# Four attention layers on one core: scores of two tiles issued together in the first stage, and the first chunk projected in blocks

## The chip, the core and the metric

The kernel runs on one core of a Trainium2 chip. The core has a matrix engine (PE in the profile; its weight loads are the row PEld), a vector engine (DVE), a scalar engine (ACT), GpSimd (POOL) and SyncE (SP), which issues transfers. The engines run at the same time, each through its own queue of instructions in order, and wait for each other through semaphores. PE writes to PSUM, eight banks of 128 x 512 float32; the other engines carry results from there to SBUF. The metric is the device time of one execution in microseconds (us).

## What is computed

```
x = x + A(layernorm(x));  x = x + B(layernorm(x))
x = x + A(layernorm(x));  x = x + B(layernorm(x))

A, B: q, k, v = x @ wqkv, 32 heads of 20 columns, S = 2048, D = 640
      p = softmax(q k^T / sqrt(20));  (p v) @ wo
A:    key k counts for query q only if 0 <= q - k < 256
B:    all keys count
```

A and B have their own weights and are each used twice. So there are four layers, 0 to 3; layers 0 and 2 are windowed, 1 and 3 full. All operands of the matmuls are bfloat16.

## The kernel before

The 2048 rows are four chunks of 512 columns (`c` = 0 to 3), and the 32 heads are eight groups of four (`g` = 0 to 7). Each head of a group has a strip of 32 partitions, of which 20 hold data. A **unit** is one layer, one chunk of queries and one group. Its scores are computed with keys on the partitions, in banks of 128 keys by up to 512 queries. A windowed unit of layer 0 has 12 banks: for each of four heads, three banks with masks. In chunk 0 these hold 512, 384 and 256 columns, in the later chunks 512.

The main loop (line 1389) goes over **tiles**. A tile is the next two or three banks of the list of units (`next_tile`, line 1344), and even and odd tiles have their own PSUM banks (line 1426). For each tile the code issues in this order: the scores on PE (line 1436); the exponential on ACT from PSUM to the tile `pt` (line 1462); some background work; the values of an earlier tile on PE (line 1495), accumulated in `op`; and the masks of the tile before on GpSimd and DVE (lines 1535 and 1546). The values come three tiles after the scores. When a unit ends, `op` goes to `on` (line 900), and tails scale it by the reciprocals of the sums.

**Background** is all that is not attention: layer norm (`t_ln`), values (`t_v`), projections of q and k (`t_block`, `t_qk_first`) and output projection (`t_out`). These are generators in the list `todo`, ordered by the unit that needs them less a lead (`push`, line 218). `background` (line 1373) advances them in every tile by a credit, 1.2 a tile while `state["unit"] < woven`; a projection costs 1.1, a piece of values 0.7. `require` (line 299) advances whatever is ahead in the list until a needed name is ready. Then `keep_clock` (line 681) adds matmuls that nobody reads (`unread`), where too little PE work was issued. While `state["unit"] < woven` (layer 0, chunks 0 and 1, sixteen units) the results of the background leave PSUM by ACT (`evac`, line 343), later by DVE.

For chunks after the first, q and k are projected in blocks of 128 columns, evacuated to a staging tile, stored to DRAM by a transfer that GpSimd issues (line 566), and read back per unit into strips of 32 partitions by eight transfers that SyncE issues (lines 802 and 803). `load_ahead` issues those of the next unit, when its blocks are ready and the buffers `qa` (4) and `ka` (18) have room. For chunk 0 of layer 0 this trip is left out: `t_qk_first` projects each group from weights that `get_w` (line 355) has spread to strips of 32 columns, with a GpSimd memset of the gaps and a DVE copy, and the evacuation goes straight to `qa` and `ka`.

The beginning is `first_ln` (line 1254): statistics of four row tiles on DVE, scale factors on GpSimd, normalization on ACT, transposes on PE, and copies to `xnT`. Filler matmuls (`warm`) stand between. Before it SyncE issues the loads of x (chunk 0), of the weights of layer 0, of x (chunks 1 to 3) and of the values' weights of the full layers. `other_constants` follows the first projection, and `t_zeros` fills buffers with zeros by transfers that GpSimd issues and then loads `wop`, the output weights.

Of the kernel before, what the change touches and what calls it, by code (L numbers as in the profile page):

```python
# [45 lines left out]
KEEP = 30  # L46
HALF = True
# [10 lines left out]
def kernel(  # L58
# [77 lines left out]
    for c in range(1, NC):  # L136
        nc.sync.dma_start(out=x_sb[:, 4 * c : 4 * c + 4, :], in_=xin[:, 4 * c : 4 * c + 4, :])
    nc.sync.dma_start(out=wv_sb[1][:], in_=wq_view[1][:, :, 2 * D : 3 * D])
# [32 lines left out]

    nc.vector.memset(ka_all[:, G:KA, :], 0.0)

    def other_constants():
        nc.vector.memset(op, 0.0)
# [3 lines left out]

# [38 lines left out]
    def push(name, gen, need, left):  # L218
        lead = 0
        if type(name) is tuple and need <= first_use(1, NC - 1, 0):  # L220
# [3 lines left out]
            if name[0] in ("k", "q"):  # L224
                lead = 7 if name[1] == 1 and name[-1] == 0 else 2

            if name[0] == "stats" or name[:2] == ("ln", 0):
                lead = 5
# [82 lines left out]
    def by_columns(out_, lhsT, rhs, start, stop):  # L311

        for j in range(4):
# [39 lines left out]
    padded = [0]  # L353

    def get_w(n, i):

        a = padded[0] % 8 * P
        padded[0] += 1
        t = wqk[:, :, a : a + P]
        tv = t.rearrange("p c (j m) -> p c j m", j=4)  # L360
        nc.gpsimd.memset(tv[:, :, :, DH:32], 0.0)
# [18 lines left out]
    def block_w(l, n, b):  # L380

        a = n * D + b * P
# [13 lines left out]
    def project(wt, xt, dst):  # L396
# [6 lines left out]
        evac(dst(), pq)  # L403
# [17 lines left out]
    def t_ln(l, c):  # L421
# [3 lines left out]
        users[l, c] = 9 if (l, c) == (0, 0) else (11, 12, 11, 11)[l]  # L425
# [50 lines left out]
    def t_v(l, c, halves):  # L476
# [9 lines left out]
        for i in range(4):  # L486
            if windowed:
# [46 lines left out]
    ka_free = deque(kas)  # L534
    qa_free = deque(qas)

    def t_qk_first(l, c, g):
# [13 lines left out]
        if g == G - 1:  # L551
            nc.sync.dma_start(out=wqk[:], in_=wq_view[1][:, :, 0 : 8 * P])
            nc.sync.dma_start(out=wqk_rest, in_=wq_view[1][:, :, 8 * P : 2 * D])
            ready.add("weights")

    def t_block(l, n, c, b):
# [5 lines left out]
        wt = block_w(l, n, b)  # L562
        yield from project(wt, xnT[l, c], staged)
        rows = slice(b * P, (b + 1) * P)
        dst = k_d[l][rows, c * C : (c + 1) * C] if n else q_d[l][c, rows, :]
        nc.gpsimd.dma_start(out=dst, in_=staging.pop())  # L566
        used(l, c)
        ready.add(("qk"[n], l, c, b))
# [68 lines left out]
    def push_layer(l, c):  # L637
# [18 lines left out]
        for g in range(G):  # L656
            for n in (0, 1):
                worder[l, n].append((n, g))
            push(("qk", l, c, g), t_qk_first(l, c, g), need[g], 2.2)
            if g == 0:  # L660
                push(("v", l, c), t_v(l, c, (0, 1)), need[0], 5.6)
# [118 lines left out]
    small_units = deque(u for u in units if u.windowed and (u.l, u.c) != (0, 0))  # L780
# [45 lines left out]
    def unit_needs(u):  # L826
        l, c, g = u.l, u.c, u.g
        if (l, c) == (0, 0):
            return [("qk", l, c, g)]
# [27 lines left out]
    def start_unit(u):  # L857
        for n in unit_needs(u):
            require(n)
        if (u.l, u.c) != (0, 0):  # L860
# [371 lines left out]
    def t_zeros():  # L1232

        z = ka_all[:, G : G + 4, :].rearrange("p a b -> p (a b)")
        yield ("wait", 4)
# [6 lines left out]
        load_wop(0, False)  # L1242
        for t in (*kts, *qts):
# [10 lines left out]
    def first_ln():  # L1254

        users[0, 0] = 9
# [9 lines left out]
        warm(14)  # L1266
# [23 lines left out]
        for i in range(4):  # L1290
# [8 lines left out]
            if i > 0:  # L1299
                trs.append(scale(i - 1))  # L1300
                warm((0, 3, 2)[i - 1])
        nc.vector.tensor_copy(out=xt[:, :, 0:P], in_=trs[0])
        trs.append(scale(3))
        warm(3)
        nc.vector.tensor_copy(out=xt[:, :, P : 2 * P], in_=trs[1])
        for n in (1, 0):
# [288 lines left out]
```

## Time and profile before

| | |
|---|---|
| time, median of 3 runs | 2161.81 us (2161.41 to 2163.21) |
| the profiled execution | 2161.74 us, span 2160.0 us |
| busy in the span | ACT 2088.0, PE 1926.8, DVE 1467.3, POOL 361.5 us |
| first projection, first exponential | at 13.26 and 16.73 us |
| evacuations leave ACT | from 148.85 us |

Times in the profile are us from the start of the span. A busy PE counts pipelined matmuls with modelled ends. A row of a group, wait or timeline names the line, the engine, the operation and the tile written and read; "x20" is a number of instructions. In the table by stretches each engine has its busy time in the stretch and its instructions, PEclk is the mean granted clock of PE, and then come the busy share of the DMA engines and their GB/s. A row of waits has the total, the number and the longest. In the timeline "SPq" is SyncE issuing, and a bracket gives the idle time before and what ended it.

### The profile page before, as it was taken

The numbers are of one execution on the slowest core, as the hardware profiler recorded it, in microseconds if no ns is written. First come the engines' busy times: TensorE is split into PE (matmuls) and PEld (weight loads), VectorE is DVE, ScalarE is ACT, GpSimd is POOL, SyncE is SP. The second block draws the span as 40 slices with busy tenths as digits, with TensorE's granted clock in tenths as the row PEclk, the third lists the DMA queues.
The fourth block names the chain that finished last, engine by engine and source line by source line (L and its number), as shares of the span: only waits on it lengthen the run. The fifth ranks groups of instructions, "written<-read, shape, count | busy, mean of one in ns | idle before, by whom it ended". The sixth has DMA issues, their size and how long they took to land. (4 is left out here: it accounts for less than half of the span.)

```text
span 2160.0 us, 73146 instructions
## 1 busy us (share of the span) xinstructions
PE 1926.8 (89%) x31790; PEld 757.8 (35%) x31791; DVE 1467.3 (68%) x2613; ACT 2088.0 (97%) x1717; POOL 361.5 (17%) x805
## 2 busy tenths in 40 slices
PE   8899999988889898888988989888898988888898
PEld 4444443433333333333333433342332222222222
DVE  6556665426666776776767743773588888987886
ACT  7889899999999999999999999999999999999997
POOL 6543434000022002400033001500000000000000
PEclk9999999999999999999999999999999999999999
DMA  6212122222110222111120122111111111111100
GB/s 204 65 54 75 54 62 69 67 63 59 55 42 27 63 53 69 38 31 48 50 83 27 33 60 75 33 45 52 54 57 44 36 36 42 32 33 39 44 27 17
DMA packets 81440, 114.33 MB, mean 53 GB/s; under 512 B 20990, under 2 KB 63070, under 8 KB 81118
## 3 DMA queue, kind: packets, MB, share of 16 engines
q1 hardware_dynamic: 71502, 81.06, 14.2%
q0 software_dynamic: 9616, 28.59, 3.8%
q8 instruction: 249, 4.08, 0.8%
q14 instruction: 73, 0.60, 0.1%
HBM read 76.58 MB, written 27.79 MB: 48 GB/s over the span
## 5 line engine op out<-in xcount | busy, mean ns | idle before, releaser
L1462 ACT ACTIVATE pt<-ps 128x1536 bf16<-128x1536 f32 (+2 forms) x1641 | 2054.0, 1417 | 38.5 <-PE ps L1436 28.9
L1436 PE MATMUL ps<-qt,kt 32*128 32x512 bf16 x3913 | 543.6, 384 | 62.8 <-ACT pt L1462 55.7
L315 PE MATMUL ps<-masks,ident 128*32 128x512 bf16 x5684 | 507.6, 384 | 94.7 <-ACT pt L1462 49.1
L1495 PE MATMUL ps<-pt,vt 128*21 128x512 bf16 x3784 | 377.1, 386 | 0.3 <-ACT pt L1462 0.2
L1436 PEld LDWEIGHTS <-kt 32*128 32x128 bf16 x3913 | 155.5, 91 | 460.1 <-issue 440.8
L315 PEld LDWEIGHTS <-ident 128*32 128x32 bf16 x5684 | 182.2, 94 | 283.4 <-issue 256.7
L1535 POOL TENSOR_SCALAR_AFFINE_SELECT pt<-pt 128x256 bf16<-128x256 bf16 (+2 forms) x508 | 219.0, 453 | 198.6 <-ACT pt L1462 185.8
L348 DVE CAST st<-ps 128x512 bf16<-128x512 f32 x134 | 92.6, 691 | 144.8 <-PE ps L315 144.5
L1495 PEld LDWEIGHTS <-vt 128*21 128x21 bf16 x3784 | 93.7, 89 | 254.2 <-issue 250.5
L315 PE MATMUL ps<-wop,on 128*32 128x320 bf16 x3712 | 160.7, 300 | 4.5 <-DVE x_sb L598 2.6
L1007 DVE TENSOR_SCALAR spare<-ps 128x512 int32<-128x512 f32 x200 | 137.2, 686 | 27.8 <-PE ps L989 24.1
L315 PEld LDWEIGHTS <-on 128*32 128x32 bf16 x5760 | 122.8, 95 | 62.3 <-issue 28.4
L1546 DVE TENSOR_TENSOR pt<-pt,masks 128x256 bf16<-128x256 bf16 (+3 forms) x270 | 117.0, 449 | 39.5 <-ACT pt L1462 37.6
L1436 PE MATMUL ps<-qa,ka 32*128 32x384 bf16 (+2 forms) x1408 | 118.5, 275 | 22.9 <-ACT pt L1462 19.6
L1203 DVE TENSOR_TENSOR on<-on,ps 128x512 bf16<-128x512 bf16 x128 | 86.4, 684 | 59.0 <-PE ps L315 56.9
L598 DVE TENSOR_TENSOR x_sb<-x_sb,ps 128x320 bf16<-128x320 bf16 x120 | 58.3, 486 | 100.3 <-PE ps L315 99.5
L315 PE MATMUL ps<-wv,xnT 128*32 128x320 bf16 x2560 | 117.1, 303 | 9.5 <-DVE on L1203 3.0
L315 PE MATMUL ps<-xnT,spare 128*32 128x512 bf16 x1720 | 118.0, 381 | 5.5 <-DVE on L1203 1.8
L315 PE MATMUL ps<-xnT,wqk 128*32 128x512 bf16 x1600 | 107.7, 381 | 4.6 <-DVE rts L1182 1.3
L1007 DVE TENSOR_SCALAR raw_o<-ps 128x512 int32<-128x512 f32 x112 | 76.8, 686 | 47.6 <-PE ps L1436 46.7
L900 DVE CAST on<-ps 128x512 bf16<-128x512 f32 x112 | 76.7, 685 | 35.5 <-PE ps L1495 28.5
L566 POOL DMA_DIRECT2D k_d<-st x75 | 41.6, 555 | 270.9 <-DVE st L348 248.0
(103 smaller groups left out, 1731.6 us busy)
## 6 DMA issues: line engine op xcount, KB each, us to landing
vt<-v_d SPq DMA_DIRECT2D x48, 336.0 KB
kt<-k_d SPq DMA_DIRECT2D x192, 80.0 KB
k_d<-st POOLq DMA_DIRECT2D x75, 128.0 KB, 2.2
q_d<-st POOLq DMA_DIRECT2D x75, 128.0 KB, 2.1
qt<-q_d SPq DMA_DIRECT2D x384, 20.0 KB
v_d<-vs POOLq DMA_DIRECT2D x16, 336.0 KB, 3.0
qa<-q_d SPq DMA_DIRECT2D x224, 20.0 KB
ka<-k_d SPq DMA_DIRECT2D x224, 20.0 KB
```

The source lines that it names most:

```text
L315: nc.tensor.matmul(out_[r], lhsT=lhsT[:, r], rhs=rhs, start=start, stop=stop)
L348: nc.vector.tensor_copy(out=out_, in_=in_)
L566: nc.gpsimd.dma_start(out=dst, in_=staging.pop())
L598: nc.vector.tensor_tensor(out=xv, in0=had, in1=yp, op=ALU.add)
L900: nc.vector.tensor_copy(out=oT, in_=op)
L1007: nc.vector.tensor_scalar(out=xi.bitcast(I32)[:, i * C : (i + 1) * C], in0=z, scalar1=SCALE * LOG2E * FIX, scalar2=127.5 * FIX, op0=ALU.mu ...
L1203: nc.vector.tensor_tensor(out=oT, in0=oT, in1=zb, op=ALU.mult)
L1436: nc.tensor.matmul(sp[:, i, col * P : (col + qn) * P], lhsT=u.k(kc, j), rhs=u.q(j, q0, qn), start=True, stop=True,)
L1462: nc.scalar.activation(out=pt[:, i:k, b0 * P :], in_=sp[:, i:k, b0 * P :], func=ACT.Exp, scale=SCALE,)
L1495: nc.tensor.matmul(op[32 * j : 32 * j + VW, q0 * P : (q0 + qn) * P], lhsT=u.v(kc, j), rhs=pg[:, i, col * P : (col + qn) * P], start=(first ...
L1535: nc.gpsimd.affine_select(out=v, in_=v, compare_op=ALU.is_gt if later else ALU.is_ge, fill=0.0, base=0, pattern=[[0, k - i], [-1 if later ...
L1546: nc.vector.tensor_tensor(out=pt_[:, i:k, cols], in0=pt_[:, i:k, cols], in1=mv_, op=ALU.mult)
```

## The change

- In the first stage (`paired()`) an even tile's scores and exponential are followed at once by those of the odd tile. Then comes what the function `rest` holds (background, values, masks), for the even tile and then for the odd one. Elsewhere the order is as before.
- In chunk 0 of layer 0 only groups 0 and 1 are projected from spread weights. Groups 2 to 7 go in four blocks (`FIRST`) by way of staging and DRAM, and are loaded like the units of later chunks. Its values are projected in two halves of 16 heads, the second with a later place in the list. `users` counts the readers of `xnT` accordingly.
- The weights of the full layers are loaded into `wqk` after the last block of q, not after group 7.
- In the beginning there are other numbers of fillers (9, then 2, 3, 3 and 4), the spread of q's weights stands ahead of the first copy to `xnT` and that of k's at the end, the first two weight tiles and two of the `qa` are cleared early, and most constants move to `t_zeros`. That task also zeroes six of the `ka`, and issues the loads of x for chunks 2 and 3 and of the full layers' values' weights, which came before the first layer norm.
- The statistics of a chunk get a lead of 12 instead of 5, and the third block of chunk 0 a lead of 1 instead of 2.

The body of `rest` is the part of the loop that was there before, moved, with one difference: values of a unit wait for the half of the projected values that they read, not for both.

```diff
--- before.py
+++ after.py
@@ -44,6 +44,7 @@
 PRE = 1.3
 PRE_1 = 0.8
 KEEP = 30
+FIRST = ((160, 288), (288, 416), (416, 544), (544, 640))
 HALF = True
 GAP_1 = 5
 QA = 4
@@ -133,9 +134,11 @@
             a = slice(n * D + a0, n * D + a1)
             nc.sync.dma_start(out=raw[:, :, a], in_=wq_view[0][:, :, a])
     nc.sync.dma_start(out=wv_sb[0][:], in_=wq_view[0][:, :, 2 * D : 3 * D])
-    for c in range(1, NC):
+
+    def load_x(c):
         nc.sync.dma_start(out=x_sb[:, 4 * c : 4 * c + 4, :], in_=xin[:, 4 * c : 4 * c + 4, :])
-    nc.sync.dma_start(out=wv_sb[1][:], in_=wq_view[1][:, :, 2 * D : 3 * D])
+
+    load_x(1)
 
     def packed(l, c):
 
@@ -169,14 +172,17 @@
             base=0, pattern=[[1 if ge else -1, P]], channel_multiplier=-1 if ge else 1,
         )
 
+    for n in range(2):
+        nc.gpsimd.memset(
+            wqk[:, :, n * P : (n + 1) * P].rearrange("p c (j m) -> p c j m", j=4)[:, :, :, DH:32], 0.0
+        )
     nc.vector.memset(ka_all[:, G:KA, :], 0.0)
-
-    def other_constants():
-        nc.vector.memset(op, 0.0)
+    nc.vector.memset(qa_all[:, 2:QA, :], 0.0)
+
+    def end_constants():
         nc.vector.tensor_copy(
             out=sel4[:], in_=ident[:].rearrange("p (j m) -> p j m", j=4)[:, :, DH]
         )
-
         nc.gpsimd.memset(spread8[:], 0.0)
         nc.gpsimd.memset(rts[:], 0.0)
         sp32 = rzp.tile([64, 2, 16], BF16, name="sp32", tag="sp32")
@@ -222,10 +228,10 @@
             chain = {"out": True, "ln": name[1] == 1, "v": name[1] == 1 and name[-1] == 0}
             lead = 5 * chain.get(name[0], False)
             if name[0] in ("k", "q"):
-                lead = 7 if name[1] == 1 and name[-1] == 0 else 2
+                lead = 7 if name[1] == 1 and name[-1] == 0 else 1 if name[1:] == (0, 0, 2) else 2
 
             if name[0] == "stats" or name[:2] == ("ln", 0):
-                lead = 5
+                lead = 12 if name[0] == "stats" else 5
         insort(todo, Task(name, gen, need, left, lead))
 
     def push_tail(name, gen):
@@ -310,7 +316,7 @@
 
     def by_columns(out_, lhsT, rhs, start, stop):
 
-        for j in range(4):
+        for j in range(lhsT.shape[-1] // 32):
             r = slice(32 * j, 32 * j + 32)
             nc.tensor.matmul(out_[r], lhsT=lhsT[:, r], rhs=rhs, start=start, stop=stop)
 
@@ -350,15 +356,19 @@
 
     wtiles = {}
     worder = {(0, n): [] for n in range(2)}
-    padded = [0]
+    padded = [2]
 
     def get_w(n, i):
 
-        a = padded[0] % 8 * P
-        padded[0] += 1
+        if i == 0:
+            a = n * P
+        else:
+            a = padded[0] % 8 * P
+            padded[0] += 1
         t = wqk[:, :, a : a + P]
         tv = t.rearrange("p c (j m) -> p c j m", j=4)
-        nc.gpsimd.memset(tv[:, :, :, DH:32], 0.0)
+        if i > 0:
+            nc.gpsimd.memset(tv[:, :, :, DH:32], 0.0)
         src = raw[:, :, n * D + 80 * i : n * D + 80 * (i + 1)]
         nc.vector.tensor_copy(
             out=tv[:, :, :, 0:DH], in_=src.rearrange("p c (j e) -> p c j e", j=4)
@@ -377,8 +387,10 @@
                 wtiles[e] = get_w(*e)
         return wt
 
-    def block_w(l, n, b):
-
+    def block_w(l, n, c, b):
+
+        if (l, c) == (0, 0):
+            return raw[:, :, n * D + FIRST[b][0] : n * D + FIRST[b][1]]
         a = n * D + b * P
         if l % 2 == 0:
             return raw[:, :, a : a + P]
@@ -400,7 +412,8 @@
             by_columns(pq, wt[:, dc, :], xt[:, dc, :], dc == 0, dc == KD - 1)
             if dc < KD - 1:
                 yield ("hold", 0.22)
-        evac(dst(), pq)
+        m = wt.shape[-1]
+        evac(dst()[0:m], pq[0:m])
         drop_m(mb)
         yield ("pe", 0.22)
 
@@ -422,7 +435,7 @@
         while ("x", l, c) not in ready:
             yield ("wait", 1)
         yield from room("xnT", "ln")
-        users[l, c] = 9 if (l, c) == (0, 0) else (11, 12, 11, 11)[l]
+        users[l, c] = (11, 12, 11, 11)[l]
         mv = mvs.pop((l, c))
         rstd = lnp.tile([P, 4], F32, name="rstd", tag="rstd")
         nc.gpsimd.tensor_scalar(
@@ -484,7 +497,7 @@
                 yield ("wait", 1)
             live["vs"] += len(halves)
         for i in range(4):
-            if windowed:
+            if windowed and 0 in halves:
                 yield from room("va")
                 va[c, i] = vap.tile([P, H, VW], BF16, name="va", tag="va")
                 nc.gpsimd.memset(va[c, i][:, :, DH : DH + 1], 1.0)
@@ -531,7 +544,7 @@
     vt = {}
     qt = {}
 
-    ka_free = deque(kas)
+    ka_free = deque(kas[0:2] + kas[G + 4 : KA] + kas[2 : G + 4])
     qa_free = deque(qas)
 
     def t_qk_first(l, c, g):
@@ -548,10 +561,12 @@
         qa[c, g], ka[c, g] = q, k
         used(l, c)
         ready.add(("qk", l, c, g))
-        if g == G - 1:
-            nc.sync.dma_start(out=wqk[:], in_=wq_view[1][:, :, 0 : 8 * P])
-            nc.sync.dma_start(out=wqk_rest, in_=wq_view[1][:, :, 8 * P : 2 * D])
-            ready.add("weights")
+
+    def load_b():
+
+        nc.sync.dma_start(out=wqk[:], in_=wq_view[1][:, :, 0 : 8 * P])
+        nc.sync.dma_start(out=wqk_rest, in_=wq_view[1][:, :, 8 * P : 2 * D])
+        ready.add("weights")
 
     def t_block(l, n, c, b):
 
@@ -559,12 +574,14 @@
             yield ("wait", 1)
         while l % 2 and "weights" not in ready:
             yield ("wait", 1)
-        wt = block_w(l, n, b)
+        wt = block_w(l, n, c, b)
         yield from project(wt, xnT[l, c], staged)
-        rows = slice(b * P, (b + 1) * P)
+        rows = slice(*FIRST[b]) if (l, c) == (0, 0) else slice(b * P, (b + 1) * P)
         dst = k_d[l][rows, c * C : (c + 1) * C] if n else q_d[l][c, rows, :]
-        nc.gpsimd.dma_start(out=dst, in_=staging.pop())
+        nc.gpsimd.dma_start(out=dst, in_=staging.pop()[0 : rows.stop - rows.start])
         used(l, c)
+        if (l, n, c, b) == (0, 0, 0, len(FIRST) - 1):
+            load_b()
         ready.add(("qk"[n], l, c, b))
 
 
@@ -653,12 +670,21 @@
                     first = need[g] if n else first
                     push(("qk"[n], l, c, b), t_block(l, n, c, b), first, 1.1)
             return
-        for g in range(G):
+        for g in range(2):
             for n in (0, 1):
                 worder[l, n].append((n, g))
-            push(("qk", l, c, g), t_qk_first(l, c, g), need[g], 2.2)
+            push(("qk", l, c, g), t_qk_first(l, c, g), 0, 2.2)
             if g == 0:
-                push(("v", l, c), t_v(l, c, (0, 1)), need[0], 5.6)
+                for n in (1, 0):
+                    push(("qk"[n], l, c, 0), t_block(l, n, c, 0), 2, 1.1)
+                push(("v", l, c, 0), t_v(l, c, (0,)), 0, 2.8)
+        for b, g in enumerate((2, 3, 5, 6)):
+            if b == 0:
+                continue
+            if b == 2:
+                push(("v", l, c, 1), t_v(l, c, (1,)), 4, 2.8)
+            for n in (1, 0):
+                push(("qk"[n], l, c, b), t_block(l, n, c, b), g, 1.1)
 
     def cool():
 
@@ -777,7 +803,7 @@
     units += [Unit(3, 0, g, PARTS[3][1]) for g in range(G)]
     units += [Unit(3, c, g) for c in range(1, NC) for g in range(G)]
     full = deque(u for u in units if not u.windowed)
-    small_units = deque(u for u in units if u.windowed and (u.l, u.c) != (0, 0))
+    small_units = deque(u for u in units if u.windowed and ((u.l, u.c) != (0, 0) or u.g >= 2))
     index = {(u.l, u.c, u.g, u.part): n for n, u in enumerate(units)}
 
     def first_use(l, c, g):
@@ -826,7 +852,13 @@
     def unit_needs(u):
         l, c, g = u.l, u.c, u.g
         if (l, c) == (0, 0):
-            return [("qk", l, c, g)]
+            if g < 2:
+                return [("qk", l, c, g)]
+            return [
+                (n, l, c, b)
+                for b, (r0, r1) in enumerate(FIRST) if r0 < 80 * (g + 1) and r1 > 80 * g
+                for n in "qk"
+            ]
         k0, k1 = key_blocks(l, u.part)
         chunks = range(k0 // 4, k1 // 4)
         blocks = range(80 * g // P, (80 * g + 79) // P + 1)
@@ -857,7 +889,7 @@
     def start_unit(u):
         for n in unit_needs(u):
             require(n)
-        if (u.l, u.c) != (0, 0):
+        if (u.l, u.c) != (0, 0) or u.g >= 2:
             ensure_loaded(u, True)
 
     def load_ahead():
@@ -1232,7 +1264,14 @@
     def t_zeros():
 
         z = ka_all[:, G : G + 4, :].rearrange("p a b -> p (a b)")
-        yield ("wait", 4)
+        yield ("wait", 3)
+        end_constants()
+        for n in (2, 5):
+            nc.gpsimd.dma_start(
+                out=ka_all[:, n : n + 3, :].rearrange("p a b -> p (a b)"), in_=z[:, 0 : 3 * C]
+            )
+        yield ("wait", 1)
+        load_x(2)
         for n in range(2):
             nc.gpsimd.dma_start(
                 out=wop[:, 4 * n : 4 * n + 3, :].rearrange("p g f -> p (g f)"), in_=z[:, 0 : 3 * D]
@@ -1240,6 +1279,10 @@
             nc.gpsimd.dma_start(out=wop[:, 4 * n + 3, :], in_=z[:, 0:D])
             yield ("wait", 1)
         load_wop(0, False)
+        yield ("wait", 8)
+        load_x(3)
+        nc.sync.dma_start(out=wv_sb[1][:], in_=wq_view[1][:, :, 2 * D : 3 * D])
+        yield ("wait", 3)
         for t in (*kts, *qts):
             nc.gpsimd.dma_start(out=t[:], in_=z[:, 0 : t.shape[1]])
             yield ("wait", 1)
@@ -1253,7 +1296,7 @@
 
     def first_ln():
 
-        users[0, 0] = 9
+        users[0, 0] = 12
         live["xnT"] += 1
         xt = take_xt(0, 0)
 
@@ -1263,7 +1306,7 @@
                     ps[:, 0, :], lhsT=ident[:], rhs=ka_all[:, G, :], start=True, stop=True
                 )
 
-        warm(14)
+        warm(9)
         rs, nm, xn = [], [], []
 
         def scale(i):
@@ -1298,15 +1341,15 @@
             nc.gpsimd.tensor_tensor(out=r[:, 0:1], in0=r[:, 0:1], in1=nhalf[:, 0:1], op=ALU.pow)
             if i > 0:
                 trs.append(scale(i - 1))
-                warm((0, 3, 2)[i - 1])
+                warm((2, 3, 3)[i - 1])
+        wtiles[0, 0] = get_w(0, 0)
         nc.vector.tensor_copy(out=xt[:, :, 0:P], in_=trs[0])
         trs.append(scale(3))
-        warm(3)
+        warm(4)
         nc.vector.tensor_copy(out=xt[:, :, P : 2 * P], in_=trs[1])
-        for n in (1, 0):
-            wtiles[n, 0] = get_w(n, 0)
         nc.vector.tensor_copy(out=xt[:, :, 2 * P : 3 * P], in_=trs[2])
         nc.scalar.copy(out=xt[:, :, 3 * P : 4 * P], in_=trs[3])
+        wtiles[1, 0] = get_w(1, 0)
         mvs.pop((0, 0))
         xnT[0, 0] = xt
         ready.add(("xnT", 0, 0))
@@ -1316,7 +1359,7 @@
         push_layer(0, 0)
         push("zeros", t_zeros(), 0, 0.0)
         require(("qk", 0, 0, 0))
-        other_constants()
+        nc.vector.memset(op, 0.0)
 
         def narrow(u):
             return u.l == 0 or (u.l == 1 and u.part in PARTS[1][:3])
@@ -1378,17 +1421,113 @@
             pump(r, r + 0.1)
             keep_clock()
 
+        closed = -2
+        masked = None
+        pts = deque()
+
+        def rest(t, n_b, cur, pt):
+
+            nonlocal closed, masked
+            if n_b and state["early"]:
+                background(t, n_b)
...
+            masked = (cur, pt) if n_b else None
+
+        def paired():
+
+            return state["unit"] < woven and len(flow) > 0
+
+        behind = None
+        cur = pt = None
         wide_pt = 0
         started = set()
-        pts = deque()
-        masked = None
         pushed = 0
         t = -1
         ended = None
-        closed = -2
         while ended is None or t < ended + 8:
             t += 1
-            state["tick"] += 1
+            state["tick"] += behind is None
             n_b = 0
             if flow:
                 if not side["early"] and state["unit"] >= index[1, 1, 0, None]:
@@ -1467,96 +1606,18 @@
                 for i, b in enumerate(cur):
                     pts.append((t, pt, i, b))
                 load_ahead()
-                if state["early"]:
-                    background(t, n_b)
             else:
                 ended = t if ended is None else ended
                 pump(2.0, 2.0)
 
...
-            masked = (cur, pt) if n_b else None
+            if n_b and t % 2 == 0 and paired():
+                behind = (t, n_b, cur, pt)
+                continue
+            if behind is not None:
+                rest(*behind)
+                state["tick"] += 1
+                behind = None
+            rest(t, n_b, cur, pt)
         mfree.update((b, (0, 0)) for b in range(1, 6))
         state["early"] = True
         while tails or todo:
```

## The prediction

> **What bounds the kernel now.** I read the page first, for which engine is full; then the busy time by stretches, cut where the profile changes character; then the waits of ScalarE inside the first stage; last the timeline of the beginning and of single tiles. The profiled execution took 2161.74 us (span 2160.0 and 1.74 around it), 0.07 below the median 2161.81, so a sum made against it stands for the median unchanged.
>
> ```profile
> PE 1926.8 (89%) x31790; PEld 757.8 (35%) x31791; DVE 1467.3 (68%) x2613; ACT 2088.0 (97%) x1717; POOL 361.5 (17%) x805
> ```
>
> ACT, the exponentials of line 1462, is the bound over the whole: it idles 72 us in 2160. The change touches only the beginning and the first stage (while `state["unit"] < woven`), so that stage decides. It ends at 148.85, where the evacuations leave ACT.
>
> ```profile
> core 0: us, PE busy (x) PEld busy (x) DVE busy (x) ACT busy (x) POOL busy (x), PEclk, DMA share, GB/s
> 0.00:16.73 16.73, 11.81 (x92) 5.08 (x96) 12.31 (x34) 6.72 (x8) 9.93 (x33) 1.00 0.94 287
> 16.73:27.00 10.27, 9.38 (x210) 5.54 (x204) 3.51 (x8) 8.05 (x16) 4.13 (x12) 1.00 0.33 110
> 27.00:50.00 23.00, 21.39 (x410) 9.31 (x414) 16.27 (x49) 20.39 (x33) 18.07 (x41) 1.00 0.59 187
> 50.00:58.00 8.00, 6.73 (x172) 3.50 (x168) 3.07 (x9) 6.43 (x12) 1.08 (x3) 1.00 0.67 210
> 58.00:85.60 27.60, 26.18 (x598) 12.94 (x586) 13.48 (x36) 23.65 (x41) 15.09 (x37) 1.00 0.22 68
> 85.60:98.00 12.40, 8.94 (x208) 4.16 (x207) 9.38 (x27) 11.13 (x12) 8.58 (x21) 0.86 0.16 43
> 98.00:118.00 20.00, 17.79 (x497) 11.01 (x493) 16.26 (x42) 13.48 (x13) 8.70 (x20) 1.00 0.08 21
> 118.00:148.85 30.85, 28.59 (x721) 14.62 (x714) 15.24 (x33) 29.30 (x38) 17.70 (x45) 1.00 0.18 57
> ```
>
> To be seen: from 16.73 to 148.85 (132.1 us) ACT is busy 112.4 and idles 19.7, over a quarter of all its idle time. In 58 to 85.6 and 98 to 118 PE is the fuller engine (95% against 86%, 89% against 67%); only in 85.6 to 98 is ACT full (90%) and PE short of work (72%). The waits of ACT in that stretch name PE too:
>
> ```profile
> ACT pt L1462 <- PE ps L1436: 6.1, 9, 1.6
> ACT st L345 <- PE ps L315: 4.3, 7, 1.4
> ACT ka L345 <- PE ps L315: 2.3, 4, 1.2
> ```
>
> So in this stage a microsecond of PE work is worth nearly a microsecond, and one of ACT work little. After the stage ACT is 98 to 99% busy for most of the way, so that a shift of the stage's end should reach the end of the kernel.
>
> **The change, part by part.**
>
> *The beginning.* The first projection starts at 13.26. Its chain:
>
> ```profile
> 3.65 5.92 PE L1262 MATMUL ps<-ka,ident 128*128 128x512 bf16 x14 [3.65 <-DVE ka L172]
> 6.55 1.98 ACT L1278 ACTIVATE xn<-x_sb,nmr,rstd 128x640 bf16<-128x640 bf16 x2 [0.97 <-DVE nmr L1272]
> 9.41 0.72 PE L1284 MATMUL ps<-ident,xn 128*128 128x128 bf16 x10
> 10.76 1.78 DVE L363 COPY wqk<-spare 128x400 bf16<-128x400 bf16 x1
> ```
>
> The first normalized tile is ready about 7.5, but the transposes sit behind 14 filler matmuls (0.42 each) until 9.57, and ACT's third tile waits 1.4 for them. With 9 fillers PE is free at 3.65 + 9 x 0.42 = 7.45. Then ACT is held by the scale factors (the fourth follows GpSimd's power, done at 9.53), its fourth tile ends about 10.6, transposes and three fillers end at 11.25, the copy by ACT (0.69) at 12.0, and the 4 fillers at 12.1: the first projection starts at 12.1 instead of 13.26, **-1.1**. The slow weight copy (1.78 against a median of 0.345) ran while GpSimd cleared `spread`; those clearings move past the start, and the copy for q fills DVE's idle 1.23 before 9.89. What is added hides: clearing two of the `qa` takes 512/2560 of 2.19 = 0.44, to 4.04, before x lands at 4.25; two weight pads (1.49/6 = 0.25 each) keep GpSimd to 5.2, before its first input at 5.47. If that cover goes, 0.5 is lost.
>
> [...] The trace has 0.42 each for the 14 fillers and 0.81 for the next three, which agrees with a late switch of rate; whether 9 are enough no run here shows.
>
> *Blocks in the first chunk.* Groups 2 to 7 lose 12 projections; 8 block projections replace them (the last pair has 96 columns, still five rounds of parallel column groups, so the same time). One costs PE 1.09 from its start to the next work (38.81 to 39.90). 4 x 1.09 = **-4.4**. ACT loses 4 evacuations of 0.59 (-2.4, counted at nothing, being beside PE). GpSimd loses 12 memsets of 0.36 (-4.3) and gains 8 stores and 2 zero copies of 0.56 (+5.6): +1.3 beside 44 us of waiting for exponentials. SyncE gains 48 loads of some 0.37 (18 us of issuing), each unit's eight taking 3.0. The splitting of the values in halves moves four pieces behind the scores of group 1, and changes no total. The loads of x chunks 2 and 3 and the second values' weights go later on SyncE; x chunk 2 is first read some 15 tiles on, so nothing waits.
>
> *Scores in pairs.* 192 banks in tiles of 3 and 2 are 77 tiles, 39 pairs. A scores block holds PE 0.32 with 3 banks and with 2:
>
> ```profile
> 101.36 0.39 PE L1495 MATMUL ps<-pt,va 128*21 128x256 bf16 x8
> 101.69 0.40 PE L1436 MATMUL ps<-qa,ka 32*128 32x256 bf16 x6
> 102.01 1.27 PE L315 MATMUL ps<-wop,on 128*32 128x320 bf16 x32
> 103.11 0.39 PE L1495 MATMUL ps<-pt,va 128*21 128x384 bf16 x8
> 103.44 0.39 PE L1436 MATMUL ps<-qa,ka 32*128 32x384 bf16 x4
> 103.76 1.27 PE L315 MATMUL ps<-wop,on 128*32 128x320 bf16 x32
> ```
>
> Five banks in four row groups need two rounds of 0.21 and one change of shape, some 0.53 instead of 0.64 (an estimate from these rows). The best end is the whole second block, 39 x 0.32 = -12.5. The worst is a loss: in ACT's queue the evacuations of the first tile's background now stand behind the second tile's exponential (1.05), and who waits is the next background on PE; PE waited five times for `xnT`, so 5 x 1.05 = +5. I take 0.1 a pair, nearest to the rows, in the three quarters of the stage that PE paces: 39 x 0.75 x 0.1 = **-2.9**. Masks come a tile later on GpSimd and DVE, but the values trail the scores by three tiles, so that stays hidden.
>
> *Order.* Statistics of the next chunk get a lead of 12 instead of 5. They now run from 82.85 and the layer norm follows at 93.74; meanwhile PE idles 3.5 and runs 28 fillers (about 2). Up to 5.5 of PE time can be filled with work taken from 98 to 118, where ACT idles 6.5; nothing at the least, since ACT is full there and takes the evacuations. I take two pieces, **-2.1**.
>
> Sum: 1.1 + 4.4 + 2.9 + 2.1 = 10.5; 2161.74 - 10.5 = **2151.2 us**. What is late next is ACT itself (112.4 less 2.4).
>
> **The rivals.**
>
> *The memory trip is late (slower).* Groups 2 to 7 now go evacuation 0.59, store issue 0.56, landing 2.1, eight loads 3.0, landing some 2: 8.3 us, plus GpSimd's queue, where each store stands behind masks that wait for exponentials. SyncE issues in order, and one wait for a store holds all later loads:
>
> ```profile
> SPq L802 <- DMA q_d<-st: 23.9, 3, 10.6
> ```
>
> Against it: by the new order a unit comes about 9 tiles (some 14 us) after its last block, and in the second chunk, on this same path, PE waited for such a load 0.2 us in all. It decides if blocks end under 8.3 us ahead. With 3 us for each of six units: 2151.2 + 18 = 2169.
>
> *The gain is absorbed (no change).* If order, pairing and projections only turn PE time into waits for evacuations behind exponentials, the start (-1.1) and ACT's 2.4 stay: 2158.2. For it: ACT is at 89 to 95% in 27 to 50 and 118 to 148.85. Against: the two stretches where PE is clearly fuller hold 47.6 us.
>
> *The clock falls.* With the rate halved through both first projections, each takes about 1.07 more, and the fillers some 0.2 each; the drop seen in 85.6 to 98 (mean clock 0.86) may come twice, about 1.7. [...] From rows: 2151.2 + 2.1 + 1.7 = 2155.
>
> *More is won.* All 5.5 of the thin stretch and 0.2 a pair: 2151.2 - 3.4 - 2.9 = 2144.9.
>
> **How the numbers follow.** Measurement can tell about 0.2% (4.3 us) from no change. Chances: forecast 0.44, clock 0.12, more 0.12 (faster 0.68); absorbed 0.14 (same); late trip 0.18 (slower). The range runs from 2143, just below the better case, to 2166, into the late case with half its waits; about 2 in 10 is outside.
>
> **What would show it.** First projection at 12.1 and first exponential near 15.6; 4 projections and 4 evacuations fewer before 148; scores of five banks in one PE block of about 0.53; ACT idle in the stage down from 19.7 to about 12, its end near 138; no PE wait on `qa` or `ka` loads over 0.5 us. Wrong would be: such waits, a rate of a half around 12 us, or a stage end that moves without the end of the kernel moving.

## The result and the profile after

| | median | runs | ratio to before, 95% interval |
|---|---|---|---|
| before | 2161.69 us (2159.39 to 2163.21) | 7 | |
| the change | 2168.52 us (2166.43 to 2168.96) | 7 | 1.0031 [1.0021, 1.0041] |

The change costs 6.8 us; 10.5 less had been forecast. Its profiled execution took 2168.48 us, span 2166.4. First the busy line of its page:

```profile
PE 1921.3 (89%) x31767; PEld 764.2 (35%) x31768; DVE 1456.4 (67%) x2592; ACT 2088.1 (96%) x1723; POOL 364.0 (17%) x803
```

PE has 5.5 us less to do and ACT as much as before, so the loss is idle time of ACT: 78.3 us in the span after 72.0. The next views say where. Rows of the busy time by stretches, first two of before, then three of the change (stretch, length, then busy time of PE, PEld, DVE, ACT, POOL, then clock, DMA share, GB/s):

```profile
0.00:160.00 160.00, 141.89 (x3104) 71.25 (x3104) 96.08 (x251) 129.36 (x176) 86.36 (x216) 0.99 0.35 108
160.00:300.00 140.00, 129.74 (x2602) 59.38 (x2594) 86.68 (x181) 127.23 (x110) 54.53 (x127) 0.98 0.24 68
```

```profile
0.00:160.00 160.00, 128.51 (x2885) 73.45 (x2885) 82.45 (x211) 116.52 (x168) 83.55 (x206) 0.96 0.41 124
80.96:98.18 17.22, 12.20 (x224) 6.41 (x226) 5.38 (x13) 8.94 (x14) 5.56 (x13) 0.70 0.14 35
160.00:300.00 140.00, 133.47 (x2766) 62.68 (x2760) 90.07 (x203) 133.55 (x119) 57.72 (x134) 1.00 0.24 68
```

At 160 us ACT has done 12.8 us less work than before (129.36 - 116.52), and PE 13.4 less: both wait. From 160 to 300 ACT does 6.3 more than before. The rest of the kernel is alike (from 300 to 2140 ACT is busy 1822.3 us before and 1822.7 after), and 12.8 - 6.3 = 6.5 is about the loss. Of the 6.3, 1.5 are evacuations: before, these are over by 149.0, and in the change they go on to 164.0. Without them the first stage loses 11.4 and 4.9 comes back behind it. So two things have to be explained, a loss in the first stage that is larger than the result and a gain behind it. The worst place of the loss is the second row, around the layer norm of chunk 2: ACT busy 52%, PE 71%, the clock at 0.70.

The waits of PE between 15.7 and 160 us (waiting line, what it waited for, total, times, longest), before and then after, tell what it waits for:

```profile
PE ps L315 <- ACT xnT L345: 2.6, 5, 1.2
PE ps L315 <- ACT st L345: 0.8, 3, 0.3
```

```profile
PE ps L321 <- ACT st L351: 7.4, 8, 1.4
PE ps L321 <- ACT xnT L351: 4.7, 4, 2.1
PE ps L321 <- ACT vs L351: 3.5, 2, 1.8
PE ps L321 <- ACT va L351: 1.7, 1, 1.7
```

All of PE's waits for ACT's evacuations (`xnT`, `st`, `vs`, `va`, `qa`, `ka`) add up to 6.2 us before and 17.8 after. In ACT's queue one sees why. The same work, projections and values of layer 0's end, in ACT's timeline before and after (start, duration, engine, line, operation, tiles, shape, number; in brackets the idle time before it and its releaser):

```profile
139.74 1.50 ACT L1462 ACTIVATE pt<-ps 128x1536 bf16<-128x1536 f32 x1
141.08 0.63 ACT L345 CAST st<-ps 128x512 bf16<-128x512 f32 x1
141.55 1.10 ACT L1462 ACTIVATE pt<-ps 128x1024 bf16<-128x1024 f32 x1
142.46 0.66 ACT L345 CAST st<-ps 128x512 bf16<-128x512 f32 x1
142.93 1.55 ACT L1462 ACTIVATE pt<-ps 128x1536 bf16<-128x1536 f32 x1
```

```profile
137.94 0.58 ACT L351 CAST st<-ps 128x512 bf16<-128x512 f32 x1
139.88 0.59 ACT L351 CAST st<-ps 128x512 bf16<-128x512 f32 x1 [1.36 <-PE ps L321]
140.47 2.37 ACT L1601 ACTIVATE pt<-ps 128x1536 bf16<-128x1536 f32 x2
142.73 0.44 ACT L351 CAST vs<-ps 128x320 bf16<-128x320 f32 x1
144.12 0.43 ACT L351 CAST vs<-ps 128x320 bf16<-128x320 f32 x1 [0.96 <-PE ps L321]
144.80 2.36 ACT L1601 ACTIVATE pt<-ps 128x1536 bf16<-128x1536 f32 x2 [0.25 <-PE ps L1575]
```

Before, one evacuation stands between two exponentials and nobody waits. After, two exponentials run together (2.37 us); only then comes the evacuation that PE waits for, and ACT in turn idles 0.96 to 1.36 until PE, set free by it, has the next piece ready. Two tiles of 3 and 2 banks and `op` leave two of the eight banks to the background, so a piece can't run ahead over a whole pair. Here 140.47 to 144.80, a pair, takes 4.3 us; before, 139.74 to 142.93 took 3.2.

### The profile page after: what moved, and what is told of

It reads as the page before. It is cut to its first block, busy times and chain, and to the rows that moved or that the text cites. A ratio compares the mean times of both kernels' runs of the same rounds, so it can differ in the third digit from the quotient of the medians.

```text
span 2166.4 us, 73185 instructions
## 1 busy us (share of the span) xinstructions
PE 1921.3 (89%) x31767; PEld 764.2 (35%) x31768; DVE 1456.4 (67%) x2592; ACT 2088.1 (96%) x1723; POOL 364.0 (17%) x803
## 5 line engine op out<-in xcount | busy, mean ns | idle before, releaser
L321 PE MATMUL ps<-masks,ident 128*32 128x512 bf16 x5752 | 514.6, 385 | 96.7 <-ACT pt L1601 49.8
L354 DVE CAST st<-ps 128x512 bf16<-128x512 f32 x126 | 87.1, 691 | 135.3 <-PE ps L321 135.0
L321 PE MATMUL ps<-xnT,spare 128*32 128x512 bf16 x1870 | 128.9, 384 | 9.4 <-ACT st L351 4.1
L1575 PE MATMUL ps<-qa,ka 32*128 32x256 bf16 (+2 forms) x1408 | 113.4, 274 | 20.1 <-ACT pt L1601 16.4
L321 PE MATMUL ps<-xnT,wqk 128*32 128x512 bf16 x1360 | 92.3, 381 | 4.0 <-ACT st L351 1.4
```

The lines of the kernel that those rows point to most:

```text
L321: nc.tensor.matmul(out_[r], lhsT=lhsT[:, r], rhs=rhs, start=start, stop=stop)
L354: nc.vector.tensor_copy(out=out_, in_=in_)
L1575: nc.tensor.matmul(sp[:, i, col * P : (col + qn) * P], lhsT=u.k(kc, j), rhs=u.q(j, q0, qn), start=True, stop=True,)
```

## The experiments

In the table each kernel is compared with runs of before that were taken together with it. "us" is the ratio less one times 2161, and differences between two kernels below are differences of that column. An interval reaches about 2 us to either side, and nearly 3 where a kernel has five runs. The stage's end is the end of the last evacuation by ACT; the last two columns are ACT's busy time in the two stretches, both from the kernel's one profiled execution.

| kernel | median (runs) | ratio, 95% interval | us | stage end | ACT 0:160 | 160:300 |
|---|---|---|---|---|---|---|
| before | | | | 149.0 | 129.4 | 127.2 |
| the change | 2168.52 (7) | 1.0031 [1.0021, 1.0041] | +6.7 | 164.0 | 116.5 | 133.6 |
| e1 change without pairs | 2159.61 (11) | 0.9998 [0.9989, 1.0007] | -0.4 | 151.8 | 130.0 | 134.2 |
| e2 change, constants early | 2165.45 (11) | 1.0023 [1.0014, 1.0032] | +5.0 | | | |
| e3 change, lead 5 | 2170.31 (5) | 1.0050 [1.0038, 1.0063] | +10.8 | | 118.6 | 127.4 |
| e4 before with pairs | 2169.38 (5) | 1.0043 [1.0030, 1.0055] | +9.3 | 155.7 | 122.0 | 127.0 |
| e5 e4, evacuation first | 2163.77 (11) | 1.0012 [1.0003, 1.0021] | +2.6 | | 127.9 | 126.3 |
| e6 before, DVE evacuates | 2165.01 (8) | 1.0024 [1.0013, 1.0035] | +5.2 | | | |
| e7 e6 with pairs | 2167.04 (5) | 1.0033 [1.0020, 1.0045] | +7.1 | | | |
| e8 e1, constants early | 2160.05 (11) | 1.0000 [0.9991, 1.0009] | 0.0 | | | |
| e9 e1 without blocks | 2153.29 (5) | 0.9966 [0.9952, 0.9979] | -7.3 | 150.8 | 132.4 | 135.6 |
| e10 change, evacuation first | 2157.86 (11) | 0.9987 [0.9978, 0.9995] | -2.8 | 155.1 | 125.5 | 134.5 |
| e11 e1, lead 5 | 2161.68 (11) | 1.0005 [0.9996, 1.0014] | +1.1 | | 125.3 | 130.7 |
| e12 e4, more fillers | 2168.79 (5) | 1.0037 [1.0024, 1.0049] | +8.0 | | | |
| e13 e1, early layer norm | 2156.17 (9) | 0.9978 [0.9968, 0.9987] | -4.8 | | 130.3 | 134.9 |
| e14 e1, early loads | 2159.55 (12) | 0.9992 [0.9983, 1.0000] | -1.7 | | | |
| e15 e9, pairs, evacuation first | 2151.45 (5) | 0.9955 [0.9943, 0.9967] | -9.7 | 148.5 | 132.8 | 135.9 |
| e16 e9, lead 5 | 2160.41 (11) | 0.9992 [0.9983, 1.0000] | -1.7 | | 131.3 | 130.0 |
| e17 e10, early layer norm | 2152.80 (5) | 0.9965 [0.9952, 0.9979] | -7.6 | 149.2 | 132.7 | 134.8 |
| e18 e15, early layer norm | 2156.87 (11) | 0.9986 [0.9978, 0.9995] | -3.0 | | 131.0 | 133.2 |

The main theory: pairs put the evacuations behind the second exponential in ACT's queue, and PE, with two background banks, waits for them. Its rivals: the clock, at 0.70 in the row around the layer norm of chunk 2; the constants, moved into the flow; the order of the statistics; the way of the blocks through DRAM. In the expectations Q is the main theory, K the clock, C what it says of the order, M the late loads, D the late layer norm of chunk 2, F and G two prices of the blocks.

### Which part costs: e1 to e4

```diff
# e1, in paired()
-            return state["unit"] < woven and len(flow) > 0
+            return False
# e2
         yield ("wait", 3)
-        end_constants()
...
         nc.vector.memset(op, 0.0)
+        end_constants()
# e3, in push
-                lead = 12 if name[0] == "stats" else 5
+                lead = 5
```

e4 is the kernel before with only the new loop (`paired`, `rest`, `behind`).

> The changed kernel with every tile's rest issued right after its own scores, as before; all else of the change kept. Theory P (the pairs cost: the background's evacuations stand behind two exponentials, PE's waits for evacuations by ACT went from 5.5 to some 17 us in the first stage): 10 us fewer than the changed kernel, about 2158, and those waits back at 6 us or less. Theory C (the constants moved into the flow and the order of the layer norms cost, pairs are harmless or help): 2168 or more.

> The changed kernel with the constants (selector, spread and its clearing) made right after the first projection, as before. Theory C: DVE's copies no longer stand behind GpSimd's clearing at 31 to 34 us, PE's wait of 2.5 and ACT's idle 2.9 near 35 to 38 go, and the half clock there: 3 to 4 us fewer, about 2165. Theory P: the hole is the price of a layer norm under pairs and comes back elsewhere: 2167 to 2169.

> The changed kernel with the lead of the statistics at 5, as before. Theory C: the hole of the layer norm at 81 to 98 us (ACT busy 8.9 of 17.2) comes from the new order and shrinks to that of before (14.8 of 17.2): about 2163. Theory P: the order is not at fault, 2167 to 2170.

> The kernel before with the pairs of the first stage alone added. Theory P: 6 to 10 us over the kernel before, 2168 to 2172, with PE's waits for evacuations by ACT up from 5.5 to some 15 us. Theory C: no more than 2162; by the prediction's sum 2159.

Taking the pairs out of the change gains 7.1 us, putting them into the kernel before loses 9.3: the pairs are the loss. In e4's profile 7.3 of it lie before 160 us (129.36 - 122.04) and 0.3 behind, and PE's waits for evacuations are 13.6 us; in e1's they are 6.6. The constants may be worth 1.7 (the intervals of the change and of e2 overlap). Nothing speaks for the theory that the new lead costs: without it the change is slower by 4.1 (the intervals just touch).

### ACT's queue or the clock: e5, e6, e7, e10, e12

The test that leaves the pairs on PE as they are and changes only ACT's order issues the background and values of the even tile ahead of the odd tile's exponential:

```diff
# e5 and e10, ahead of the loop over the exponentials
+                if behind is not None:
+                    rest(*behind)
+                    state["tick"] += 1
+                    behind = None
                 i = 0
# e6, and e7 with the pairs of e4
-                        state["act"] = state["unit"] < woven
+                        state["act"] = False
# e12
-            state["least"] = (1.76 if state["unit"] >= woven else 1.0) * n_b / 3
+            state["least"] = 1.76 * n_b / 3
```

> Pairs alone, with one thing moved in ACT's queue: the odd tile's exponential is issued after the even tile's rest, so that evacuations of the first background stand ahead of it; PE's order (both scores, then both rests) is that of the pairs. Theory Q (the cost is the evacuation behind two exponentials): the 8.8 us that pairs alone cost go for the most part, 2159 to 2163, PE's waits for ACT's evacuations fall from 12 to 6 us or less. Theory R (the cost lies in PE's own order: two backgrounds and values in a row leave ACT without scores): 2168 or more.

> The kernel before, with the background's results taken from PSUM by DVE in the first stage too, no pairs. The base for the next run. ACT loses some 37 us of evacuations there, DVE gains them beside masks and statistics. No theory at stake; within 15 us of the kernel before.

> The run before this one with pairs added. Evacuations no longer stand in ACT's queue. Theory Q: pairs cost little or nothing against the run without them (under 3 us, perhaps a gain of 3). Theory R: they cost 6 to 10 us here too.

The pairs' cost falls from 9.3 to 2.6, and PE's waits for evacuations from 13.6 us to 6.2, the value of before. The largest of them, first in e4, then in e5:

```profile
PE ps L315 <- ACT xnT L345: 6.3, 5, 1.9
PE ps L315 <- ACT xnT L345: 2.7, 4, 1.2
```

Where DVE evacuates, pairs cost 1.9 (7.1 - 5.2), within the intervals. So the place of the evacuations in ACT's queue costs, and not PE's order. What is left with a mended queue may be that values and masks still come a tile later; that wasn't separated.

> The whole change with the odd tile's exponential issued after the even tile's rest. If the queue on ACT is what the pairs cost in the changed kernel too: some 6 us fewer than the changed kernel, 2161 to 2164. If in the changed kernel the cost is in the layer norm's place and the constants: 2166 or more.

In the change itself the same move gains 9.5 us, more than the 6 expected, and PE's waits for evacuations fall from 17.8 to 9.2. ACT's timeline in e10, with the columns as above:

```profile
141.66 1.45 ACT L1605 ACTIVATE pt<-ps 128x1536 bf16<-128x1536 f32 x1
143.00 0.58 ACT L351 CAST st<-ps 128x512 bf16<-128x512 f32 x1
143.47 1.04 ACT L1605 ACTIVATE pt<-ps 128x1024 bf16<-128x1024 f32 x1
144.38 0.61 ACT L351 CAST st<-ps 128x512 bf16<-128x512 f32 x1
```

Exponential and evacuation alternate again, nobody waits here, and a pair takes 3.3 us (141.66 to 144.93).

> Pairs alone on the kernel before, with the fillers' bound in the first stage raised from 1.0 to 1.76 (the bound of the later stages). Theory K (what pairs cost is the halved clock: 20.5 us of it in the profile against 10.2 before): the half clock in the first stage goes and with it 4 us or more, 2162 to 2165. Theory Q (the evacuations behind two exponentials): no better than 2167, the fillers cost as much as they save.

More fillers change nothing that can be told (8.0 against 9.3), though they took away only half of what they were meant to: in the first 160 us PE is at half rate for 13.7 us in e4's profile and for 6.8 in e12's, and PE's waits for evacuations stay at 13.6. e5 says more. Its profile has as much half rate as e4's, 20.5 us in all (an episode that the end of the span cuts is left out here), and yet the pairs' cost is mostly gone. So the clock is no cause of the loss. The profile of before has 10.2 us of half rate, the change's 13.7.

### The constants without the pairs: e8

The edit of e2 made to e1.

> The changed kernel without pairs and with the constants right after the first projection. If the constants in the flow cost 3 us by themselves, as in the run with pairs, 2156 to 2157, and faster than the kernel before; if their cost needs the pairs (a mask late for values that come in a bunch), 2159 to 2160.

0.0 against -0.4: nothing. What the constants may cost in the change is perhaps a tile's mask that comes late beside a pair, which was not separated; alone they are covered.

### The blocks: e9, e13, e14

```diff
# e9, on e1
-        for g in range(2):
+        for g in range(G):
...
-            push(("qk", l, c, g), t_qk_first(l, c, g), 0, 2.2)
+            push(("qk", l, c, g), t_qk_first(l, c, g), need[g], 2.2)
# e13, on e1
-                lead = 12 if name[0] == "stats" else 5
+                lead = 12 if name[0] == "stats" or name == ("ln", 0, 2) else 5
# e14, on e1
-    load_x(1)
+    for c in range(1, NC):
+        load_x(c)
+    nc.sync.dma_start(out=wv_sb[1][:], in_=wq_view[1][:, :, 2 * D : 3 * D])
```

In e9 all groups are projected from spread weights as before, the values in one piece, and the weights of the full layers are loaded after group 7.

> The changed kernel without pairs and without the blocks: all eight groups of the first chunk from spread weights as before; the new beginning, the later loads and constants and the lead of 12 stay. Theory F (the four projections saved are no gain in time, because the tiles they free are filled with pieces of later chunks whose evacuations then fall to ACT: 76 evacuations by ACT in the first stage against 70 before): within 2 us of the run without pairs, 2158 to 2162. Theory G (PE work removed counts, as the prediction had it, 4.4 us): 2163 to 2165.

Neither theory had this: without the blocks the kernel gains 6.9 more. The blocks save two evacuations by ACT and not four: e1 has 76 where e9 has 78, and with a lead of 5 it is 68 in e11 where e16 has 70. Part of the credit that the blocks free is spent on later chunks' pieces (24 of their `st` in e1, 22 in e9), and these leave by ACT instead of later by DVE. That before has only 70 comes with its lead of 5, as e16 shows. And the number of evacuations is not what the blocks cost: e9 has more of them and is faster.

> The changed kernel without pairs, blocks kept, with the layer norm of chunk 2 given a lead of 12 as its statistics have, so that it runs beside the projections of chunk 1. Theory D (the four projections saved are given back at that layer norm, for which no other background is left): unit 8 ends some 4 us earlier and the time is 2153 to 2156. Theory M (the blocks cost through the trip to DRAM and SyncE's queue): 2158 to 2161.

> The changed kernel without pairs, blocks kept, with the loads of x (chunks 2 and 3) and of the full layers' values' weights back in the beginning. Theory M: they no longer fall between the units' loads near 60 to 81 us, 2 to 5 us fewer, 2155 to 2158. Theory D: 2159 to 2161, or worse if they slow the beginning.

An earlier layer norm of chunk 2 gives back 4.4 of the 6.9, nearly what its theory said; but the eighth unit ended at 90.95 where e1's ended at 90.49, so not by way of the unit it named. Loads issued early, with the queue of SyncE as before, gain 1.3 with overlapping intervals, so the late loads are not shown to cost anything. In e1's profile, between 15.7 and 160 us, PE's weight loads wait 0.6 us for transfers to `ka`, and ACT waits once, 0.8, for a store.

### Together: e15 to e18

e15 is e9 with the pairs and the move of e5; e16 is e9 with the lead of e3; e17 is e10 and e18 is e15, both with the lead of e13. e11 is e1 with the lead of e3: if the early statistics win 2.1 us, as predicted, 2161 to 2163 had been expected of it, and 2158 to 2161 if they only move the work. It took 2161.68, 1.5 more than e1, with overlapping intervals.

> No blocks, pairs with the odd tile's exponential behind the even tile's rest. If the pairs' own order on PE costs some 2.5 us, as with pairs alone: 2155 to 2157. If the merged scores gain once ACT's queue is mended: 2150 to 2153.

> No pairs, no blocks, lead of the statistics at 5: what is left is the beginning, with the later loads and constants. If the 7.6 us come mostly from the order of the statistics: 2158 to 2160. If from the beginning: 2153 to 2156.

> The whole change, with the odd tile's exponential behind the even tile's rest and the layer norm of chunk 2 with a lead of 12. If the two repairs add up (6 to 10 us and 3 us on the changed kernel): 2152 to 2156. If the second finds nothing left to mend: 2157 to 2159.

> The same without the blocks. If the blocks still cost: 3 us or more under the run before this one, 2149 to 2152. If what they cost was only the place of the layer norm: within 1.5 us of it.

e15 is the fastest, 2151.45 us (2150.83 to 2153.22), ratio 0.9955 [0.9943, 0.9967]. Its pairs, with a mended queue, are worth 2.4 over e9, within the intervals. e17, the change with two small edits, is 14.3 faster than the change. e18 fits neither of its expectations and refutes the reading that the blocks have a fixed price: the early layer norm that helps with blocks (4.8 from e10 to e17) costs 6.7 without (e15 to e18). With it the blocks are 4.6 ahead, without it 6.9 behind. The intervals of e17 just touch those of e10 and e18; the other two steps are clear of them.

## Why the prediction was wrong

Four kernels make a ladder from before to the change, one term a rung, to be set beside the terms of the sum:

| term | predicted | measured | from |
|---|---|---|---|
| beginning | -1.1 | -1.7 | e16 |
| order of statistics | -2.1 | -5.6 | e9 less e16 |
| blocks in the first chunk | -4.4 | +6.9 | e1 less e9 |
| scores in pairs | -2.9 | +7.1 | change less e1 |
| sum | -10.5 | +6.7 | |

Two rungs depend on the path. The order of statistics is worth 5.6 without blocks and pairs, 1.5 with the blocks (e1 less e11, overlapping intervals) and 4.1 in the whole change (change less e3); the blocks cost 6.9 with a lead of 12 and 2.8 with one of 5 (e11 less e16, overlapping intervals).

**The beginning** was right: the first projection and the first exponential start 1.0 earlier than before. The -1.7 of e16 has the moved constants and loads in it too, and its interval reaches to no change. The timeline of the change (predicted 12.1 and 15.6):

```profile
12.22 2.34 PE L321 MATMUL ps<-xnT,wqk 128*32 128x512 bf16 x40
15.70 1.45 ACT L1601 ACTIVATE pt<-ps 128x1536 bf16<-128x1536 f32 x1 [0.50 <-PE ps L1575]
```

Both projections together take 2.34 us, as at 13.26 before, so the rate with nine fillers was the same. The 2.1 that the rival of the falling clock adds for half rate in both projections is shown by no run.

**Scores in pairs** is the first step that failed, and it failed in its worst end. The gain on PE is as computed. Timeline of the change, scores of five banks and what follows:

```profile
149.18 0.60 PE L1575 MATMUL ps<-qa,ka 32*128 32x128 bf16 x10
149.72 1.26 PE L321 MATMUL ps<-xnT,wqk 128*32 128x512 bf16 x20
```

0.54 from start to start; 0.53 had been estimated. The loss was named too, evacuations that stand behind the second exponential, but its size was taken from the waits that PE already had: five for `xnT`, 5 x 1.05 = +5. That row counts who was late before. In the pair every evacuation of the even tile's background comes an exponential later, and whether PE notices is a matter of free banks. With the pairs alone (e4) the five waits for `xnT` grew by 3.7 us, which the estimate covers, and those for `st`, `vs`, `qa` and `va` by another 3.7, which it left out. In the change the waits for `st` grew from 0.8 to 7.4 and for `vs` from 0.7 to 3.5; PE's waits for evacuations grew by 11.6 us in all, over twice the worst end, and ACT idles in them too. The error was then made worse by the choice: between -12.5 and +5 I took the gain, though the price of a wrong queue had no ceiling from a row. Where the queue is put right, pairs gain 2.4 (e10 against e1, e15 against e9), near the 2.9 of the sum but within the intervals; in e5 they still cost 2.6.

**Blocks in the first chunk** failed in its sign, and e1 with e9 shows that it did so without the pairs. The step that failed is to take four projections less for 4.4 us of time. PE does make four fewer, but the background runs by credit, and the list fills part of the room again: two of the four evacuations saved come back as other pieces. That is not the price, since e9 has more evacuations than e1. The price goes by the order of the list, and with the lead of one layer norm the medians even turn (e17 and e18). By which wait the blocks lose in e1 is open: of the 2.4 us that ACT has done less than in e9 at 160, 2.1 lie in 80 to 92, around that layer norm, but e13 did not bring the unit there forward. It is not the clock: in both profiles its mean is 1.00 in every stretch up to 300 us. The executions of e1 spread from 2156.0 to 2162.0, and its profile is the fastest, only 2.7 above that of e9, so it does not show the loss in full.

**Order** was right in sign, and 2.1 lies within the 1.5 to 5.6 that it is worth by the path; the place was wrong. I looked for it in 82 to 118. The table's last column has it: kernels with a lead of 5 have 126 to 131 us of ACT work between 160 and 300, those with 12 have 133 to 136. There was room: before, ACT idles 12.8 us in these 140, a stretch that the prediction passes over with "98 to 99% busy for most of the way". PE's wait for `on` between 200 and 300 is 3.3 us in before and in e16, 1.0 in the change, 0.7 in e9. By the condition in `push` the lead holds for the statistics of layers 0 and 1, and I applied it to the one chunk that I was looking at. This is the gain that hid 4.9 of the first stage's 11.4.

**Constants** had no term: of the clearing of `spread` the prediction says that it moves past the start, and nothing of what it meets there. The timeline of the change:

```profile
31.27 1.70 DVE L183 COPY sel<-ident 128x4 bf16<-128x4 bf16 x1
31.63 1.35 DVE L192 COPY sp<-ident 32x32 bf16<-32x32 bf16 x1
32.00 0.94 POOL L186 MEMSET spread<- 128x1024 bf16 x1
```

At 14.37 before, the two copies took 0.15 each. DVE's next mask comes at 34.67, GpSimd's at 35.85, behind the clearings, zero copies and a layer norm's scale factors, and PE idles 2.55 up to 36.30; in e2 the same wait is 1.24. In the change this may cost 1.7, without pairs nothing (e8). That the pairs took a cover that was there is likely and not shown.

**What carries a stage's end to the end of the kernel** held: e4 has 7.3 us of ACT work less at 160, and its profiled execution is 7.3 longer (2169.01 - 2161.74). But "a microsecond of PE work is worth nearly a microsecond" did not: PE had less work, and the end came later.

**The rivals.** The late memory trip gave nearly the measured time (2169), but that is luck, as its reason did not occur: it priced six units at 3 us each, and in the stage PE's weight loads waited 0.6 us for transfers to `ka`, PE's matmuls not at all. At the start both projections took the 2.34 us of before, and the clock's falls in the stage, 13.7 us at half rate, are not the cause, going by e5. A rival with the right mechanism was in the text, as the +5 of a term, and was given neither its own chance nor its real price. The sign to look for, a rate of a half or waits on loads, was therefore the wrong one.

## What to carry to other kernels

Before an in-order engine gets a second long instruction ahead of short ones, list every short one behind it and the buffers that they free: with two banks, one exponential of 1.05 us more in front made PE's waits for evacuations 13.6 us out of 6.2 (e4). Bound such a cost by all instructions that are moved behind, not by the waits of today, which count only those that were late already. In a kernel that fills its gaps from a list, removed work is first of all room that the list can fill again, and an order rule acts wherever its name occurs: look at every stage for it.

## What the runs showed of the hardware

- The granted clock went from 1.00 to 0.50 and back in steps. In the change an evacuation of `xnT` stands behind two exponentials, PE idles 2.10 us for it, and the clock is at 0.50 from 93.83 to 97.24, through most of the next two projections:

```profile
91.14 2.37 ACT L1601 ACTIVATE pt<-ps 128x1536 bf16<-128x1536 f32 x2
93.39 0.71 ACT L351 COPY xnT<-ps 128x640 bf16<-128x640 bf16 x1
94.15 3.84 PE L321 MATMUL ps<-xnT,spare 128*32 128x512 bf16 x40 [2.10 <-ACT xnT L351]
```

3.84 us for 40 matmuls that took 2.34 at 12.22. The half-rate episodes in the profiles of before and the change last 3.41 us or twice that, where the end of the span does not cut them. Those of before start at 94.55, 217.43 and 278.87; the distances, 122.88 and 61.44 us, are about 36 and 18 times 3.41. In the 3.41 us before the fall at 93.83 in the change PE was busy 1.63; ahead of the fall at 94.55 in before it was busy 2.05. What makes the clock fall is not shown.
- Two small DVE copies, at 31.27 and 31.63 in the change, took 1.70 and 1.35 us instead of 0.15 while GpSimd ran two masks (from 31.38) and the clearing of `spread` (from 32.00), and both end within 0.05 of the end of that clearing (32.94). In e1 the same two took 1.00 and 0.93, in e2, where they run at 12.09 and 12.10, 0.15 each. What held them is not shown.
